# A windowed attention with sinks and a max-out FFN on one core: half-height score tiles, 32-wide sink tiles, crossbar transposes and another prologue

## The chip, the cores and the metric

The kernel runs on one core of a Trainium2 chip. The metric is the device time of one execution in microseconds (us). The engines are TensorE (PE; PEld is its weight load), VectorE (DVE), ScalarE (ACT), GpSimd (POOL) and SyncE (SP), which here only issues DMAs.

## The reference

```python
B, H, S, D = 4, 8, 768, 64            # n_sink = 4, window = 128
scores = q @ k.T / sqrt(D)
keep = (pos_k < 4) | ((0 <= pos_q - pos_k) & (pos_q - pos_k < 128))
a = softmax(where(keep, scores, -1e9))
x = (a @ v) as [B*S, H*D]             # 3072 x 512
h = max(x @ w1, x @ w2, x @ w3)       # each w is 512 x 768
out = h @ w_out                       # 768 x 512, float32
```

Inputs and output are float32; the kernel multiplies in bf16. No maximum is subtracted before the exp, and the sum over a row comes from a column of ones beside V.

## The kernel before, in words

The work is cut into 12 chunks of 256 query rows with all 8 heads, three chunks for each batch (`c` = 0, 1, 2). A chunk passes these steps, each a function with a letter in the order strings of `run` (L333):

- `load` (L59): four 256 KB DMAs of K and Q halves and four 128 KB DMAs of V, all on SP. `cast_qk` (L163) and `cast_v` (L171) make bf16 of them, on POOL but for the first two chunks.
- K and Q (`prep`, L185): 16 TensorE transposes (L192) into PSUM. Q is copied by ACT (L195), K by DVE (L200) into `kb`, a block-diagonal form: for two heads, 64 keys each, 128 rows and columns with zeros off the diagonal. The zeros are written once by `zeros` (L94), mostly on POOL. For the first chunk of a batch, small DVE copies (L208) put the four sink keys into `ks`.
- S (`score`, L214): eight tiles of 128 x 512 a chunk, a matmul of 128, one of 256 and one of 128 columns for each, an exp by ACT (L232), and for every second tile a multiplication by a 0/1 mask on DVE (L234). Z (`sink_score`, L236): four matmuls of 256 columns added into one tile, in chunks with c > 0.
- A (`av`, L249): for each half of the heads and each 128 queries one matmul for the sinks (260 columns) and eight of 130 columns (L263), against a V that is padded with zeros for the other head. DVE normalises (L268, L271). The sinks' V rows come from eight small DMAs (L84) and POOL products (L154).
- T (`xpose`, L276): four TensorE transposes of x for each 128 rows (L282) and an ACT copy (L283).
- F (`ffn_h`, L287): nine groups a chunk, each eight matmuls of 256 columns (L294); the first of three weights is copied by ACT (L298), the others are maximised in by DVE (L300).
- Y (`ffn_y`, L302): six matmuls of 512 columns (L305), an ACT copy (L308) and a DMA to the output on SP (L310), twice a chunk.

Every engine works through its instructions in the order of the program text, SP too. The first chunks (L339 to L377) have an order written out by hand; weights are loaded by POOL's queue, three matrices together for a range of columns, between POOL's casts and memsets. Then a loop over i = 2 to 11 (L379) casts chunk i+2, loads chunk i+3 and runs one string, which mixes the FFN of chunk i, the attention of chunk i+1 and the K and Q transposes of chunk i+2:

```python
run("Sb0 Fa0 Sb1 Kc0 Fa1 Sb2 Kc1 Fa2 Sb3 Fa3 Zb Sb4 Fa4 Ab00 Sb5 Fa5 Ab01 Sb6 Qc0 Fa6 "
    "Sb7 Qc1 Fa7 Fa8 Ab10 Ab11 Ya0 Tb0 Tb1 Ya1", a=i, b=i + 1, c=i + 2)
```

PSUM has two banks for scores, two for transposes and AV, four for the FFN.

Of the kernel before, what the change touches and what calls it, by code (L numbers as in the profile page):

```python
# [15 lines left out]
def kernel(  # L17
# [12 lines left out]
):  # L30
    nc = tc.nc
# [14 lines left out]

    with tc.manual_schedule():
        const = tc.alloc_tile_pool(name="const", bufs=1)  # L50
        raw = tc.alloc_tile_pool(name="raw", bufs=2)
        work = tc.alloc_tile_pool(name="work", bufs=2)
        ps_s = tc.alloc_tile_pool(name="ps_s", bufs=2, space=bass.MemoryType.PSUM)
        ps_o = tc.alloc_tile_pool(name="ps_o", bufs=2, space=bass.MemoryType.PSUM)
        ps_f = tc.alloc_tile_pool(name="ps_f", bufs=4, space=bass.MemoryType.PSUM)

        raws = {}

        def load(ci, gate=None):  # L59

            b, c = divmod(ci, CPB)
            t0 = c * 256
            eng = nc.sync
            qk = raw.tile([128, 2, H, 2, D], F32, tag="qk_raw", name="qk_raw")
            vr = raw.tile([128, 2, NP, 2, D], F32, tag="v_raw", name="v_raw")
            if gate is not None:
                gate.memset(qk[0:1, 0, 0, 0, 0:1], 0.0)
            for g in range(2):
                for j, src in ((0, k), (1, q)):
                    eng.dma_start(  # L70
                        out=qk[:, j, 4 * g:4 * g + 4],
                        in_=src[b, 4 * g:4 * g + 4, t0:t0 + 256].rearrange("h (p i) d -> p h (i d)", i=2))
            for h in range(2):
                for n in range(2):
                    eng.dma_start(
                        out=vr[64 * h:64 * h + 64, n],
                        in_=v[b, h::2, t0 + 128 * n:t0 + 128 * n + 128]
                            .rearrange("a (r i) d -> r a (i d)", i=2))
            raws[ci] = (qk, vr)

        load(0)
        vs_raw = const.tile([H * n_sink, B, D], F32, name="vs_raw")
        for h in range(H):
            nc.sync.dma_start(out=vs_raw[h * n_sink:(h + 1) * n_sink],  # L84
                              in_=v[:, h, 0:n_sink].rearrange("b s d -> s b d"))


        kb_sb = [const.tile([128, CPB, 2, NP, 2, 128], BF16, name=f"kb{i}") for i in range(2)]
        qT = [const.tile([128, NP, S], BF16, name=f"qT{i}") for i in range(2)]
        vb_sb = [const.tile([128, CPB, 2, NP, 2, 2, D + 1], BF16, name=f"vb{i}") for i in range(2)]  # L90
        ks = [const.tile([128, NP * 136], BF16, name=f"ks{i}") for i in range(2)]
        vs = const.tile([128, B, H, D + 1], BF16, name="vs")

        def zeros(i, c, eng):  # L94
            for h in range(2):
                hp = slice(64 * h, 64 * h + 64)
                eng.memset(kb_sb[i][hp, c, :, :, :, 64 - 64 * h:128 - 64 * h], 0.0)  # L97
                eng.memset(vb_sb[i][hp, c, :, :, :, 1 - h], 0.0)
                eng.memset(vb_sb[i][hp, c, :, :, :, h, D:D + 1], 1.0)

        zeros(0, 0, nc.vector)
        nc.vector.memset(ks[0], 0.0)
        nc.vector.memset(ks[1], 0.0)

        ident = const.tile([128, 128], BF16, name="ident")
        make_identity(nc, ident)

        msk = const.tile([128, 2, 4, 128], BF16, name="msk")
        nc.gpsimd.memset(msk[:, :, 0:2], 1.0)
        for h in range(2):  # L110
            hp = slice(64 * h, 64 * h + 64)
            nc.gpsimd.affine_select(
                out=msk[hp, :, 1], in_=msk[hp, :, 1], compare_op=ALU.is_ge, fill=0.0,
                base=0, pattern=[[-1, 2], [1, 128]], channel_multiplier=-2)
            nc.gpsimd.affine_select(
                out=msk[hp, :, 0], in_=msk[hp, :, 0], compare_op=ALU.is_gt, fill=0.0,
                base=0, pattern=[[1, 2], [-1, 128]], channel_multiplier=2)
        nc.gpsimd.tensor_copy(msk[:, :, 2:4], msk[:, :, 0:2])
        msk0 = const.tile([128, 2, 3, 128], BF16, name="msk0")
        nc.gpsimd.tensor_copy(msk0, msk[:, :, 1:4])  # L120
        for h in range(2):
            nc.gpsimd.memset(msk0[64 * h:64 * h + n_sink // 2, :, 0:2], 1.0)

        w_sb = {}

        def load_w(fo, fn):
            for wi, w in enumerate((moe_w1, moe_w2, moe_w3)):
                wt = const.tile([128, DS, fn], BF16, name=f"w{wi}_{fo}")
                nc.gpsimd.dma_start(
                    out=wt, in_=w[:, fo:fo + fn].rearrange("(a p) f -> p a f", p=128))  # L130
                for f in range(fn // 128):
                    w_sb[wi, fo // 128 + f] = wt[:, :, f * 128:(f + 1) * 128]

        wo = const.tile([128, FB, d_model], BF16, name="wo")

        def load_wo():
            for a in range(2):
                nc.gpsimd.dma_start(
                    out=wo[:, 3 * a:3 * a + 3],
                    in_=moe_w_out[384 * a:384 * a + 384].rearrange("(a p) f -> p a f", p=128))  # L140


        R = H * n_sink
        bm = const.tile([R, H], F32, name="bm")

        def sink_v_init():
            nc.gpsimd.memset(bm, 1.0)
            nc.gpsimd.affine_select(out=bm, in_=bm, compare_op=ALU.is_ge, fill=0.0, base=0,
                                    pattern=[[-n_sink, H]], channel_multiplier=1)
            nc.gpsimd.affine_select(out=bm, in_=bm, compare_op=ALU.is_ge, fill=0.0,  # L150
                                    base=n_sink - 1, pattern=[[n_sink, H]], channel_multiplier=-1)
            nc.gpsimd.memset(vs, 0.0)

        def sink_v(b):  # L154
            nc.gpsimd.tensor_tensor(
                out=vs[0:R, b, :, 0:D],
                in0=vs_raw[:, b].unsqueeze(1).to_broadcast([R, H, D]),
                in1=bm.unsqueeze(2).to_broadcast([R, H, D]), op=ALU.mult)
            nc.gpsimd.tensor_copy(vs[0:R, b, :, D:D + 1], bm.unsqueeze(2))

        bfs = {}

        def cast_qk(ci, j, g, eng):  # L163
            qk = raws[ci][0]
            if ci not in bfs:
                bfs[ci] = raw.tile([128, 2, 2, 2, 256], BF16, tag="qk_bf", name="qk_bf")
            eng.tensor_copy(  # L167
                bfs[ci][:, j, g].rearrange("p i (h d) -> p h i d", d=D),
                qk[:, j, 4 * g:4 * g + 4])

        def cast_v(ci, h):  # L171
            b, c = divmod(ci, CPB)
            vr = raws[ci][1]
            hp = slice(64 * h, 64 * h + 64)
            nc.gpsimd.tensor_copy(  # L175
                vb_sb[b % 2][hp, c, :, :, :, h, 0:D].rearrange("p n a i d -> p (n a i) d"),
                vr[hp].rearrange("p n a i d -> p (n a i) d"))

        def cast(ci):
            for j, g in ((0, 0), (1, 0), (0, 1), (1, 1)):  # L180
                cast_qk(ci, j, g, nc.gpsimd)
            for h in range(2):
                cast_v(ci, h)

        def prep(ci, j, g):  # L185

            b, c = divmod(ci, CPB)
            x = bfs[ci]
            pt = ps_o.tile([128, 2, 2, 128], BF16, tag="o", name="pt")
            for i in range(2):  # L190
                for p in range(2):
                    nc.tensor.transpose(pt[:, i, p], x[:, j, g, i, p * 128:(p + 1) * 128], ident)  # L192
            if j == 1:
                dst = qT[b % 2][:, 2 * g:2 * g + 2, c * 256:c * 256 + 256]
                nc.scalar.copy(dst.rearrange("p a (t i) -> p i a t", i=2), pt)  # L195
            else:
                kb = kb_sb[b % 2]
                for h in range(2):
                    hp = slice(64 * h, 64 * h + 64)
                    nc.vector.tensor_copy(  # L200
                        kb[hp, c, :, 2 * g:2 * g + 2, :, 64 * h:64 * h + 64]
                            .rearrange("p i a n r -> p i (a n) r"),
                        pt[hp].rearrange("p i a (n r) -> p i (a n) r", r=64))
                if c == 0:
                    kv = ks[b % 2].rearrange("p (a y) -> p a y", y=136)
                    for h in range(2):
                        for i in range(2):
                            nc.vector.tensor_copy(  # L208
# [215 lines left out]
```

## Time and profile before

| | us |
|---|---|
| median of 3 runs | 236.91 (236.32 to 238.7) |
| span of the profiled execution | 235.6 |
| PE busy | 203.3 |
| DVE busy | 140.4 |
| ACT busy | 115.1 |
| POOL busy | 91.8 |

The profile is one execution; its times count from the start of its span. Besides the page, this text uses four views. The groups of instructions give, for one line of the kernel and one operation, the busy time, the mean duration of one, and the idle time ahead of them with what ended it. The chain of waits is the sequence of work that ended last, followed back from the end: start, length, engine, tile and line. The timeline lists the instructions of one engine or queue: start, length, engine, line, operation, with the wait ahead of it in brackets. The table by stage lists for a stretch of time the busy time of PE, PEld, DVE, ACT and POOL, then the granted TensorE clock, the busy share of the DMA engines and GB/s. Matmuls overlap each other in time, so the spacing of their starts, and not the mean duration, is what one costs.

### The profile page before, as it was taken

To read this page: it belongs to the slowest core of one execution; us is meant where nothing else is said; L and a number is where in the kernel's file an instruction comes from. 1 tells how busy PE (TensorE), PEld (TensorE's weight loads), DVE (VectorE), ACT (ScalarE), POOL (GpSimd) and SP (SyncE) were. 2 spreads that over 40 slices of the span, in tenths; PEclk is the share of its full clock that TensorE was granted. 3 is DMA by queue.
4 is the path that set the end of the run, shared out by engine and by line. 5 is a ranking of instruction groups with operands and counts; after the bars stand their busy time and mean duration, and the time that the engine had idled before them with its cause. 6 is when DMAs were issued, how large, how long until landed. Compare 5 with 4: busy or idle time off the path is not lost.

```text
span 235.6 us, 4953 instructions
## 1 busy us (share of the span) xinstructions
PE 203.3 (86%) x1956; PEld 163.9 (70%) x1968; DVE 140.4 (60%) x314; ACT 115.1 (49%) x213; POOL 91.8 (39%) x129
## 2 busy tenths in 40 slices
PE   0647876989944999999899999998999999999993
PEld 0434655877533868978778869877978689799781
DVE  7737674456342973855856739729629648547350
ACT  2622363257450457546446555464564466473411
POOL 8599961699468650621602502603404300000000
PEclk9999999999997999999999999999999999999998
DMA  6599199682699904907607519139039020010202
GB/s 171 101 134 239 32 161 259 118 120 58 182 278 233 232 18 142 218 3 234 122 22 236 105 63 266 30 101 251 10 107 248 4 89 4 25 66 0 92 0 89
DMA packets 46006, 28.66 MB, mean 122 GB/s; under 512 B 2208, under 2 KB 42912, under 8 KB 45984
## 3 DMA queue, kind: packets, MB, share of 16 engines
q1 hardware_dynamic: 42016, 25.21, 43.4%
q0 software_dynamic: 3968, 3.15, 9.0%
q8 instruction: 15, 0.25, 0.5%
q14 instruction: 7, 0.06, 0.1%
HBM read 25.20 MB, written 6.29 MB: 134 GB/s over the span
## 4 chain that ended last, share of the span: by engine, by line
PE 57%; DVE 13%; POOL 9%; DMA 7%; ACT 5%; issue 4%; SPq 3%; POOLq 0%; DVEq 0%; ACTq 0%
PE h_ps L294 29%; PE y_ps L305 10%; PE o_ps L263 6%; DMA v_raw<-in_v_dram 4%; DVE e_sb L234 4%; DVE h_sb L300 4%; DMA w<-in_moe_w_dram 3%; PE st L224 3%; ACT e_sb L232 3%; PE pt L192 2%; DVE kb L200 2%; PE xt_ps L282 2%; POOL vb L175 2%; SPq L70 2%; POOL kb L97 2%
## 5 line engine op out<-in xcount | busy, mean ns | idle before, releaser
L294 PE MATMUL h_ps<-xT,w 128*128 128x256 bf16 x864 | 111.0, 278 | 2.2 <-DMA w<-in_moe_w_dram 1.5
L294 PEld LDWEIGHTS <-w 128*128 128x128 bf16 x864 | 82.7, 100 | 13.1 <-DMA w<-in_moe_w_dram 2.0
L232 ACT ACTIVATE e_sb<-st 128x512 bf16<-128x512 f32 (+1 forms) x96 | 53.5, 564 | 44.2 <-PE st L226 44.2
L234 DVE TENSOR_TENSOR e_sb<-e_sb,msk 128x1024 bf16<-128x1024 bf16 (+1 forms) x48 | 36.6, 762 | 56.0 <-ACT e_sb L232 55.9
L300 DVE TENSOR_TENSOR h_sb<-h_sb,h_ps 128x512 bf16<-128x512 bf16 x72 | 49.3, 685 | 15.6 <-PE h_ps L294 13.3
L167 POOL CAST qk_bf<-qk_raw 128x512 bf16<-128x512 f32 x40 | 24.9, 627 | 82.0 <-DMA qk_raw<-in_k_dram 71.1
L263 PE MATMUL o_ps<-vb,e_sb 128*128 128x130 bf16 x352 | 30.8, 227 | 6.8 <-DVE e_sb L234 4.0
L305 PE MATMUL y_ps<-wo,h_sb 128*128 128x512 bf16 x132 | 32.7, 379 | 0.6
L263 PEld LDWEIGHTS <-e_sb 128*128 128x128 bf16 x352 | 24.8, 100 | 10.5 <-DVE e_sb L234 6.2
L308 ACT COPY y_sb<-y_ps 128x512 f32<-128x512 f32 x24 | 14.0, 585 | 35.6 <-PE y_ps L305 32.1
L175 POOL CAST vb<-v_raw 64x1024 bf16<-64x1024 f32 x24 | 26.5, 1104 | 9.5 <-DMA v_raw<-in_v_dram 6.1
L192 PE MATMUL pt<-ident,qk_bf 128*128 128x128 bf16 x192 | 19.4, 230 | 12.1 <-DVE qk_bf L167 5.5
L298 ACT CAST h_sb<-h_ps 128x512 bf16<-128x512 f32 x36 | 21.1, 585 | 15.8 <-PE h_ps L294 15.6
L224 PE MATMUL st<-qT,kb 128*128 128x256 bf16 x96 | 27.0, 285 | 1.6 <-ACT qT L195 0.8
L200 DVE COPY kb<-pt 64x512 bf16<-64x512 bf16 x48 | 20.1, 419 | 6.9 <-PE pt L192 6.3
L192 PEld LDWEIGHTS <-qk_bf 128*128 128x128 bf16 x192 | 13.6, 102 | 14.4 <-POOL qk_bf L167 7.1
L195 ACT COPY qT<-pt 128x512 bf16<-128x512 bf16 x24 | 17.7, 737 | 11.5 <-PE pt L192 11.5
L226 PE MATMUL st<-qT,kb 128*128 128x128 bf16 x96 | 21.9, 228 | 0.0
L271 DVE TENSOR_TENSOR x_sb<-o_ps,rc 128x256 bf16<-128x256 f32 x48 | 20.4, 425 | 1.7
L305 PEld LDWEIGHTS <-h_sb 128*128 128x128 bf16 x144 | 13.0, 98 | 11.9 <-DVE h_sb L300 1.2
L283 ACT COPY xT<-xt_ps 128x512 bf16<-128x512 bf16 x24 | 13.2, 595 | 9.0 <-PE xt_ps L282 9.0
L222 PE MATMUL st<-qT,kb 128*128 128x128 bf16 x64 | 14.0, 218 | 0.9 <-ACT qT L195 0.8
(43 smaller groups left out, 130.7 us busy)
## 6 DMA issues: line engine op xcount, KB each, us to landing
qk_raw<-in_k_dram SPq DMA_DIRECT2D x24, 256.0 KB
qk_raw<-in_q_dram SPq DMA_DIRECT2D x24, 256.0 KB
v_raw<-in_v_dram SPq DMA_DIRECT2D x48, 128.0 KB
out_dram<-y_sb SPq DMA_DIRECT2D x24, 256.0 KB
w<-in_moe_w_dram POOLq DMA_DIRECT2D x3, 512.0 KB, 7.4
w<-in_moe_w_dram POOLq DMA_DIRECT2D x3, 256.0 KB, 4.9
wo<-in_moe_w_out_dram POOLq DMA_DIRECT2D x2, 384.0 KB, 5.6
vs_raw<-in_v_dram SPq DMA_DIRECT2D x8, 4.0 KB
```

The source lines that it names most:

```text
L167: eng.tensor_copy(bfs[ci][:, j, g].rearrange("p i (h d) -> p h i d", d=D), qk[:, j, 4 * g:4 * g + 4])
L175: nc.gpsimd.tensor_copy(vb_sb[b % 2][hp, c, :, :, :, h, 0:D].rearrange("p n a i d -> p (n a i) d"), vr[hp].rearrange("p n a i d -> p (n a ...
L192: nc.tensor.transpose(pt[:, i, p], x[:, j, g, i, p * 128:(p + 1) * 128], ident)
L200: nc.vector.tensor_copy(kb[hp, c, :, 2 * g:2 * g + 2, :, 64 * h:64 * h + 64] .rearrange("p i a n r -> p i (a n) r"), pt[hp].rearrange("p i ...
L224: nc.tensor.matmul(st[:, 1:3], lhsT=kb[:, c, i, p, 0], rhs=qh[:, q0:q0 + 256], start=True, stop=True)
L226: nc.tensor.matmul(st[:, 3], lhsT=kb[:, c, i, p, 1], rhs=qh[:, q0 + 128:q0 + 256], start=True, stop=True)
L232: nc.scalar.activation(e[:, i, lo:], st[:, lo:], AF.Exp, scale=scale)
L234: nc.vector.tensor_mul(e[:, :, lo:], e[:, :, lo:], msk if c > 0 else msk0)
L263: nc.tensor.matmul(o[:, 2 * a:2 * a + 2], lhsT=es[ci, p][:, i, sl], rhs=vb_sb[b % 2][:, n // 2, n % 2, p, i], start=(c == 0 and x == 0), s ...
L294: nc.tensor.matmul(hp[:, f], lhsT=w_sb[wi, 2 * fp + f][:, ds], rhs=xTs[ci][:, ds, :], start=(ds == 0), stop=(ds == DS - 1))
L300: nc.vector.tensor_max(dst, dst, hp)
L305: nc.tensor.matmul(yp, lhsT=hs[ci][:, fb, t * 128:(t + 1) * 128], rhs=wo[:, fb], start=(fb == 0), stop=(fb == FB - 1))
```

## The change

- K is no longer padded. `kT` holds 128 rows (two heads of 64) and 128 keys; a score tile is for one head and uses 64 of the 128 rows of the array, the two heads of a pair one after the other in the two halves. The number of tiles, exps and masks stays. V is no longer padded either: AV is a matmul of 65 columns for each head, query half and key block, 32 (c > 0) a chunk as before.
- The sinks stand in four column strips of 32: the sink scores of a pair of heads go to their own 32 partitions, and AV's sink matmuls read eight rows of such a strip. The sinks' V rows come from V by a selection matmul.
- Three DMAs load a chunk (K, Q, V of 512 KB each); `raw` and `work` have three buffers, and PSUM is one pool of eight banks that all tiles use in turn.
- K and Q of chunks 0 and 1 are transposed by TensorE from float32, those of chunks 2 and 3 from bf16; from chunk 4 on `turn_xbar` has SP issue DMA transposes, two for K and one for Q. From chunk 4 on x is transposed by two DMAs (`xpose_xbar`), which SP issues as well.
- The prologue works on two chunks. The weights are requested matrix by matrix, starting after the first part of chunk 1's K has landed, and the FFN of chunks 0 and 1 goes matrix by matrix too. A few matmuls on zeros are put at the start.
- The loop runs over i = 4 to 11. AV of chunk i+1 opens it, the scores of chunk i+2 follow four FFN groups, and y is that of chunk i-1. A y tile is stored by two DMAs.

The core of the diff (added lines, shortened):

```python
+    KQ_XBAR = 4
+    X_XBAR = 4
...
+        def turn32(ci, t, g, eng):
+            pt = bank([128, 2, 2, 128], F32, f"{t}t32")
+            x = raws[ci][t]
+            for a in range(2):
+                for i in range(2):
+                    for h in range(2):
+                        nc.tensor.matmul(pt[64 * h:64 * h + 64, a, i],
+                                         lhsT=x[:, 2 * (2 * g + a) + h, i], rhs=id32,
+                                         start=True, stop=True, skip_group_check=True)
...
+        def turn_xbar(ci):
+            x = bfs[ci, "k"].rearrange("p a i h d -> p (a i h d)")
+            for n in range(2):
+                nc.sync.dma_start_transpose(
+                    out=kT[ci % 4][:, n].rearrange("p a i r -> p (a i) r"),
+                    in_=x[64 * n:64 * n + 64])
+            nc.sync.dma_start_transpose(
+                out=qT[ci % 3].rearrange("p a i n r -> p (a i) (n r)"),
+                in_=bfs[ci, "q"].rearrange("p a i h d -> p (a i h d)"))
...
+        def sink_score(ci):
...
+            for p in range(NP):
+                nc.tensor.matmul(st[32 * p:32 * p + 32], lhsT=ks[b % 2][:, p],
+                                 rhs=q_ap(ci, p, None), start=True, stop=True,
+                                 skip_group_check=True)
...
+        def score(ci, p):
...
+            for what in range(lo, 4):
+                if what == 2:
+                    continue
                 for h in range(2):
                     hp = slice(64 * h, 64 * h + 64)
+                    kk = kT[(ci - (what == 0)) % 4][hp, int(what != 1), p].rearrange("p i r -> p (i r)")
+                    qq = q_ap(ci, p, {0: 0, 1: None, 3: 1}[what])[hp]
...
+                    nc.tensor.matmul(o, lhsT=kk, rhs=qq, start=True, stop=True)
...
+        def av(ci, pairs, eng=None):
...
+            if c:
+                for t in range(2):
+                    for p in pairs:
+                        pp = slice(32 * p, 32 * p + 2 * n_sink)
+                        nc.tensor.matmul(o[p][:, t], lhsT=es[ci, "sink"][pp, t], rhs=vs[b % 2][pp],
+                                         start=(t == 0), stop=False, skip_group_check=True)
+            for p in pairs:
...
+                        for h in range(2):
+                            nc.tensor.matmul(
+                                o[p][:, t, h], lhsT=es[ci, p][:, h, s],
+                                rhs=vb[(CPB * b + n // 2) % 4][:, n % 2, 2 * p + h],
+                                start=first, stop=(s == 2 * t + 1), skip_group_check=True)
...
+        def xpose_xbar(ci):
+            for t in range(2):
+                nc.sync.dma_start_transpose(
+                    out=xT_of(ci)[:, :, t * 128:(t + 1) * 128],
+                    in_=xs[ci][:, t].rearrange("p h d -> p (h d)"))
...
+        def attend(ci):
...
+            av(ci, range(NP))
+            if ci >= X_XBAR:
+                xpose_xbar(ci)
...
+        cast(3)
+        load_all(4)
+        for n in range(5):
+            F(2, n)
+        scores(3)
+        cast(4)
+        load_all(5)
+        turn_xbar(4)
+        F(2, 5)
...
+        attend(3)
+        ffn_y(2, 0)
+        T(3)
+        ffn_y(2, 1)
+        cast(5)
+        load_all(6)
+        turn_xbar(5)
+        scores(4)
...
+        for i in range(4, NCH):
             attend(i + 1)
             if i + 2 < NCH:
                 cast(i + 2)
             load_all(i + 3)
+            for n in range(4):
+                F(i, n)
+            if i + 2 < NCH:
+                turn_xbar(i + 2)
+            scores(i + 2)
+            ffn_y(i - 1, 0)
+            masks(i + 2, [0])
+            ffn_y(i - 1, 1)
+            masks(i + 2, [1])
+            F(i, 4)
+            masks(i + 2, [2])
+            F(i, 5)
+            masks(i + 2, [3])
+            F(i, 6)
+            F(i, 7)
+            F(i, 8)
+        ffn_y(NCH - 1, 0)
+        ffn_y(NCH - 1, 1, last=True)
```

`load_all(ci)` issues the three loads of a chunk, `cast(ci)` the eight casts on POOL, `scores(ci)` the sink scores and the four pairs' scores (ahead of them, for chunks below 4, the TensorE transposes), `F(i, n)` one FFN group, `masks` the multiplications by the mask. Chunk 2's load is held by `gate` and `wait_for` until the first part of the third FFN weight has landed.

## The prediction

> **What bounds the kernel now.** I read the page's busy shares first, then the groups of instructions, the chain that ended last, and last the timeline of single queues in the loop.
>
> ```profile
> PE 203.3 (86%) x1956; PEld 163.9 (70%) x1968; DVE 140.4 (60%) x314; ACT 115.1 (49%) x213; POOL 91.8 (39%) x129
> PEclk9999999999997999999999999999999999999998
> q1 hardware_dynamic: 42016, 25.21, 43.4%
> L294 PE MATMUL h_ps<-xT,w 128*128 128x256 bf16 x864 | 111.0, 278 | 2.2 <-DMA w<-in_moe_w_dram 1.5
> ```
>
> TensorE is the bound, and all DMAs of SP lie on one queue, q1. It is busy 43.4% of 235.6 us, 102 us, for 25.21 MB: 247 GB/s while it works. Matmuls overlap, so I take spacings from the chain of waits: eight FFN matmuls of 256 columns last 0.87 us (0.109 each), eight of 128 or 130 columns 0.46 (0.057), six y matmuls 1.30.
>
> ```profile
> 104.55 0.61 PE xt_ps L282 x8
> 121.92 0.45 PE xt_ps L282 x8
> 154.43 0.45 PE xt_ps L282 x8
> 172.02 0.45 PE xt_ps L282 x8
> 204.30 0.45 PE xt_ps L282 x8
> 219.69 0.45 PE xt_ps L282 x8
> ```
>
> This piece closes an iteration of the loop. From 104.55 to 204.30 six of them (chunks 4 to 9) take 99.75 us, 16.6 each. TensorE's own work for a chunk that is not first in its batch is 72 x 0.109 = 7.85 (FFN), 2.6 (y), 8 x 0.223 = 1.78 (scores), 0.44 (sink scores), 2.3 (AV), 0.46 (x) and 0.92 (K, Q) = 16.35. So the loop is dense. With about 1.7 us of y and copies behind 104.55, the span splits into 106.3 up to that loop, 99.8 in it and 29.5 behind.
>
> The early part has the idle time, and one of its stalls shows what the change will meet again:
>
> ```profile
> 73.83 0.61 PE L192 MATMUL pt<-ident,qk_bf 128*128 128x128 bf16 x4 [4.41 <-POOL qk_bf L167]
> 74.23 1.92 PE L294 MATMUL h_ps<-xT,w 128*128 128x256 bf16 x8
> 79.02 1.04 PE L294 MATMUL h_ps<-xT,w 128*128 128x256 bf16 x8
> ```
>
> ```profile
> 72.00:74.00 2.00, 0.17 (x2) 0.17 (x3) 0.00 (x0) 0.00 (x0) 2.00 (x5) 0.95 1.23 257
> 74.00:75.00 1.00, 1.00 (x8) 0.82 (x7) 0.51 (x2) 0.00 (x0) 0.88 (x2) 0.50 1.24 164
> 76.00:77.00 1.00, 1.00 (x9) 0.88 (x8) 0.76 (x2) 0.49 (x1) 0.38 (x1) 0.50 1.24 176
> 77.00:78.00 1.00, 1.00 (x11) 0.86 (x10) 0.77 (x2) 0.00 (x0) 0.88 (x1) 0.90 1.18 261
> ```
>
> After a wait of 4.41 us the granted clock (third column from the right) is 0.50 for three microseconds: eight matmuls take 1.92 instead of 1.04, and about 1.5 us go on top of the wait.
>
> ```profile
> 107.57 0.39 SPq L70 DMA_DIRECT2D qk_raw<-in_k_dram  x1
> 110.76 0.61 POOL L167 CAST qk_bf<-qk_raw 128x512 bf16<-128x512 f32 x1 [9.07 <-DMA qk_raw<-in_k_dram]
> 112.64 0.61 POOL L167 CAST qk_bf<-qk_raw 128x512 bf16<-128x512 f32 x1 [0.47 <-DMA qk_raw<-in_k_dram]
> 114.24 0.61 POOL L167 CAST qk_bf<-qk_raw 128x512 bf16<-128x512 f32 x1 [0.98 <-DMA qk_raw<-in_q_dram]
> 115.35 2.56 POOL L175 CAST vb<-v_raw 64x1024 bf16<-64x1024 f32 x2 [0.50 <-DMA v_raw<-in_v_dram]
> ```
>
> A chunk's load (1.57 MB) lands in the order of its issue: the first piece 2.8 us after its issue ends at 107.96, the last 7.7 us after the first issue. And SP issues in program order: it waits 129 us in all for y copies, with the loads queued behind them.
>
> **The change, part by part.**
>
> *Early part.* The block-diagonal K goes, and with it POOL's memsets (10 x 0.96, 10 x 0.97, 10 x 0.19: 21 us); the eight small sink loads (4.9 us of SP) and POOL's sink products (4.7) go too. FFN weights are requested right after chunk 1's first half, so the 7.4 us wait for w in the chain shrinks. What is new: 64 fp32 transposes for chunks 0 and 1, which no row shows. Bounds are the 128-column spacing 0.057 and, for operands twice as wide in several passes, 0.32 (above the 512-column 0.216); I take 0.16, nearer the short row, since half an output tile is written at a time: 10 us, partly under loads. Chunk 0's fourth piece lands at 8.33 (a DVE wait), so at 0.9 to 1.0 us a piece chunk 1's Q lands at 12 to 13. Two more transposes, a copy and a score bring FFN to 19 us, where the first weights (4.5 to 9.3 us after issue at about 11) are there too; bounds 15 and 25. From there to the y tiles of chunk 1: 18 FFN groups 15.7, y 5.2, scores 3.2, AV 3.8, transposes 1.8 = 29.7, and 2 for gaps: 51. On to chunk 4's loop: FFN 15.7, y 2.6, scores 4.2, AV 2.9, transposes 1.4 = 26.8, and 3 for the first crossbar chunk, whose request lies behind load 5: 81 us, against 106.3. Bounds 71 and 90.
>
> *Scores, sinks, AV.* A score tile costs 0.223 as before if its two 64-row halves follow each other, half if they run side by side: 1.78 or 0.9 a chunk, taken at 1.3; sink scores 0.44 or 0.1, taken at 0.3. AV halves its columns but keeps all 32 weight loads: 2.3 or 1.0, taken at 1.9. The Trainium skill, page "TensorEngine Tiling (Array Packing)", section Key Properties, speaks against it: changing the tiling mode drains the engine. No row here has such a switch; at an assumed 0.2 us for six switches a chunk the sum would be 14 us longer, without it as given here.
>
> *K, Q and x by DMA.* TensorE loses 0.92 + 0.46 a chunk, DVE the K copies (4 x 0.42), ACT 2 x 0.74 + 2 x 0.60. Neither is the bound: in the loop ACT keeps nine exps of 0.4 to 0.6, three h and two y copies (8 us), DVE four masks, six maxima and four normalisations (9.5). SP gains five issues a chunk, two more y stores and loses five load issues. The order on SP in iteration i is: x(i+1) twice, load i+3, K(i+2) twice and Q(i+2), then y stores; TensorE's is AV(i+1), four FFN groups, scores(i+2), y, five FFN groups. Counted from the start of AV:
> - x(i+1) is normalised at 3.3: DVE ends its last max at 0.9, then four times 0.176 + 0.425. SP, waiting for it, has load, K and Q behind it.
> - The x requests end at 4.4 (0.5 each, the load row; y stores show 0.36), the load lands at 4.4 + 7.7 = 12.1.
> - K and Q, 0.52 MB behind it on q1, need 2.1 at q1's 247 GB/s: 14.2. The low bound is no queueing: issues end at 7.6, plus 2.8, is 10.4. The high bound is a crossbar several times slower than a copy, 3 us or more for each 256 KB. The copy row is the nearest, as the bytes and the queue are the same.
> - TensorE reaches the scores at 1.9 + 4 x 0.87 = 5.4 and waits 8.8, twice the stall above: the clock halves, 1.5 more.
> - Behind it: sinks and scores 1.6, y 2.6, five FFN groups 4.4 = 8.6.
>
> T = 14.2 + 8.6 + 1.5 = 24.3. Five iterations (4 to 8) 121.5; iteration 9 loads nothing: 6.0 + 2.8 = 8.8, T = 8.8 + 8.6 + 0.8 = 18.2. Together 139.7, against 99.8.
>
> Two pages differ on the crossbar. "Advanced Engine Details and Errata", section X-Bar Transpose (TRN2), has it as fast as a plain copy, 350 to 400 GB/s: the sum would be 3 us shorter. "VectorE: DVE Perf Modes", section The three transpose paths, gives 1309 ns for a 128x128 block: as an estimate, 16 blocks one after the other are 21 us behind the load, and the sum passes 340.
>
> *Casts.* POOL's 4.7 us a chunk stay (V in four pieces), one iteration ahead of need: nothing, while the load lands before the next iteration's start.
>
> *End.* Iteration 10: AV 1.9, FFN 7.85, y 2.6; iteration 11: 10.45, then y 2.6 and the 3.5 us from the last matmul to the end: 28.9, against 29.5.
>
> **Sum.** 81 + 139.7 + 28.9 = 249.6, against the profile's span of 235.6; the median of the runs shown lies 1.3 above that span: 251 us.
>
> **Rivals.**
> 1. *Faster: K and Q do not queue behind the load's data.* Then they land at 10.4, T = 20.5, and 81 + 102.5 + 18.2 + 28.9 + 1.3 = 232. For it: SP has issued them by 7.6, and the load leaves the queue idle half of each period. Against: the landing order above. It decides at a landing by 10.9 us; with the low bounds of early part, scores and AV and no drop of the clock it gives 71 + 5 x 18.4 + 16.8 + 27.5 + 1.3 = 209.
> 2. *Slower still: the crossbar is the bound.* At 3 us for each 256 KB (x, K, Q) instead of 1.05, six iterations take 4 to 6 us more: 280. For it: no row shows a 2-byte transposing transfer; against: the bytes are only a third of the load's.
> 3. *The half tiles do not run side by side, or the switches cost:* 0.5 to 1.2 us a chunk over twelve chunks: 257 to 265. For it: the number of weight loads stays, and scores lie behind the wait, where nothing hides them; against: AV lies ahead of it and would be hidden.
>
> **How the numbers follow.** About 1% is what a measurement of this kernel can tell from no change. My forecast has 0.50 (own range 240 to 260; 0.48 slower, 0.02 the same). Rival 1 has 0.34 (0.30 faster, 0.04 the same), since the gain ahead of the loop, 25 us, is safe and the loss rests on one queue's order. Rival 2 has 0.11, rival 3 0.05 (0.04 slower, 0.01 the same). That is 0.30, 0.07 and 0.63. The range 219 to 263 leaves out rival 1's lowest and most of rival 2.
>
> **What would show it.** Right: iterations of 22 to 26 us in which TensorE waits 7 to 10 us ahead of the scores, for a DMA of kT or qT issued behind x and the load, with a granted clock of 0.5 behind the wait; FFN starting near 19 us; loop 4 starting near 81. Wrong: score matmuls that start without a wait, iterations under 19 us, or the wait on another engine. If x is ready well before 3.3, or SP issues the load ahead of it, the forecast falls.

## The result, and the profile after

| | before | after |
|---|---|---|
| median, us | 236.82 (236.32 to 238.7) | 272.5 (271.53 to 274.65) |
| ratio to before, 95% interval | | 1.1511 [1.144, 1.1582] |
| span of the profiled execution | 235.6 | 269.6 |
| PE busy | 203.3 | 186.8 |
| loop: first AV of iteration 4 | | 85.0 |
| six iterations 4 to 9 | 99.8 | 154.6 |

The kernel is 15% slower. The direction and the place were predicted; the forecast, 251, was 21.5 us too low, and the measured time lies outside its range (219 to 263). Two of the runs below, e6 and e7, were profiled in an execution that was slower than others of the same kernel, so their profiles are not used to compare times of iterations.

The page of the kernel after: busy shares, clock by slices, the load queue, the FFN group, and the transposing DMAs (issuer, count, median us to landing).

```profile
PE 186.8 (69%) x1934; PEld 138.2 (51%) x1946; DVE 115.1 (43%) x251; ACT 90.8 (34%) x177; POOL 64.3 (24%) x130
PEclk9999999999999965995599579757975798699998
q1 hardware_dynamic: 67152, 31.34, 52.3%
L352 PE MATMUL h_ps<-xT,w 128*128 128x256 bf16 x864 | 99.1, 273 | 1.2 <-ACT xT L335 1.1
...
kT<-k_bf SPq DMA_TRANSPOSE x16, 4.5
xT<-x_sb SPq DMA_TRANSPOSE x16, 2.5
qT<-q_bf SPq DMA_TRANSPOSE x8, 3.4
```

TensorE has 16.5 us less work and is idle 83 us. The first 14 slices (94 us) have a full clock; the dips begin with the loop. The waits of TensorE say where (total us, times, longest):

```profile
PE sk L254 <- DMA qT<-q_bf: 42.5, 6, 11.6
PE st L279 <- DMA qT<-q_bf: 22.2, 2, 11.4
```

64.7 us in eight waits, all for the transposed Q; the two shortest, 1.4 and 0.8 us, lie ahead of the loop. One iteration (i = 6, AV starts at 139.75), TensorE's timeline and then SP's, with the cast on POOL that starts when V has landed:

```profile
139.75 0.29 PE L302 MATMUL o_ps<-vs,e_sink 8*128 8x130 bf16 x8
...
140.99 3.66 PE L352 MATMUL h_ps<-xT,w 128*128 128x256 bf16 x32
155.28 0.41 PE L254 MATMUL sk<-qT,ks 128*32 128x256 bf16 x4 [10.64 <-DMA qT<-q_bf]
155.62 1.89 PE L279 MATMUL st<-qT,kT 64*128 64x128 bf16 x24
...
160.47 4.53 PE L352 MATMUL h_ps<-xT,w 128*128 128x256 bf16 x40
164.93 0.29 PE L302 MATMUL o_ps<-vs,e_sink 8*128 8x130 bf16 x8
```

```profile
142.80 2.54 SPq L339 DMA_TRANSPOSE xT<-x_sb  x2
145.39 0.58 SPq L78 DMA_DIRECT2D k_raw<-in_k_dram  x1
146.02 0.57 SPq L78 DMA_DIRECT2D q_raw<-in_q_dram  x1
146.64 1.12 SPq L78 DMA_DIRECT2D v_raw<-in_v_dram  x1
147.85 3.85 SPq L217 DMA_TRANSPOSE kT<-k_bf  x2
151.80 1.34 SPq L220 DMA_TRANSPOSE qT<-q_bf  x1
153.53 2.62 POOL L181 CAST vb<-v_raw 64x512 bf16<-64x512 f32 x4 [0.71 <-DMA v_raw<-in_v_dram]
```

SP has nothing to issue until x is ready, 3.05 us after the start of AV, and then issues without a break for 10.3 us; Q's request is out 13.4 us after the start of AV, Q lands at 15.5, and TensorE has stood still since 4.9. The table by stage shows what the wait does to the clock (third column from the right):

```profile
145.00:148.00 3.00, 0.00 (x0) 0.00 (x0) 0.00 (x0) 0.26 (x1) 0.00 (x0) 1.00 0.49 106
148.00:149.00 1.00, 0.00 (x0) 0.00 (x0) 0.00 (x0) 0.00 (x0) 0.00 (x0) 0.55 1.15 346
149.00:153.00 4.00, 0.00 (x0) 0.00 (x0) 0.00 (x0) 0.00 (x0) 2.34 (x4) 0.50 1.25 289
156.00:157.00 1.00, 1.00 (x20) 0.88 (x18) 0.00 (x0) 0.86 (x3) 0.14 (x1) 0.50 0.06 16
158.00:159.00 1.00, 0.78 (x5) 0.38 (x4) 0.71 (x2) 1.00 (x3) 0.00 (x0) 0.83 0.00 0
```

It halves 3.5 us into the wait and comes back 3 us after its end, so the 24 score matmuls take 1.89 us (1.06 in runs below where the clock behind the wait is 1.00).

### The profile page after: what moved, and what is told of

Read it like the earlier page. It is cut to its first block, busy times and chain, and to the rows that moved or that the text cites. A ratio compares the mean times of both kernels' runs of the same rounds, so it can differ in the third digit from the quotient of the medians.

```text
span 269.6 us, 4874 instructions
## 1 busy us (share of the span) xinstructions
PE 186.8 (69%) x1934; PEld 138.2 (51%) x1946; DVE 115.1 (43%) x251; ACT 90.8 (34%) x177; POOL 64.3 (24%) x130
## 4 chain that ended last, share of the span: by engine, by line
PE 54%; DMA 25%; SPq 6%; DVE 5%; ACT 5%; issue 3%; POOL 1%; ACTq 0%; DVEq 0%; POOLq 0%
PE h_ps L352 27%; DMA q_raw<-in_q_dram 14%; PE y_ps L363 13%; DMA qT<-q_bf 10%; PE st L279 5%; SPq L339 4%; PE o_ps L311 3%; ACT e_sb L281 3%; PE kt L200 2%; PE qt L200 2%; DVE e_sb L287 2%; DVE h_sb L358 1%; DMA k_raw<-in_k_dram 1%; SPq L78 1%; SPq L217 1%
## 5 line engine op out<-in xcount | busy, mean ns | idle before, releaser
L352 PE MATMUL h_ps<-xT,w 128*128 128x256 bf16 x864 | 99.1, 273 | 1.2 <-ACT xT L335 1.1
L352 PEld LDWEIGHTS <-w 128*128 128x128 bf16 x864 | 83.5, 98 | 13.4 <-issue 2.1
L281 ACT ACTIVATE e_sb<-st 128x512 bf16<-128x512 f32 (+1 forms) x96 | 45.6, 586 | 27.3 <-PE st L279 26.9
L287 DVE TENSOR_TENSOR e_sb<-e_sb,msk 128x1024 bf16<-128x1024 bf16 x32 | 21.8, 696 | 58.1 <-ACT e_sb L281 58.0
L178 POOL CAST k_bf<-k_raw 128x512 bf16<-128x512 f32 x20 | 11.9, 622 | 112.8 <-DMA k_raw<-in_k_dram 97.4
L181 POOL CAST vb<-v_raw 64x512 bf16<-64x512 f32 x48 | 30.5, 636 | 18.3 <-DMA v_raw<-in_v_dram 16.3
L279 PE MATMUL st<-qT,kT 64*128 64x128 bf16 (+1 forms) x256 | 17.7, 293 | 24.1 <-DMA qT<-q_bf 22.2
L363 PEld LDWEIGHTS <-h_sb 128*128 128x128 bf16 x144 | 15.2, 112 | 21.9 <-issue 11.9
L279 PEld LDWEIGHTS <-kT 64*128 64x128 bf16 x256 | 11.8, 117 | 28.4 <-issue 26.2
L369 ACT COPY y_sb<-y_ps 128x512 f32<-128x512 f32 x23 | 13.6, 601 | 17.7 <-PE y_ps L363 13.2
L311 PE MATMUL o_ps<-vb,e_sb 128*128 128x65 bf16 x352 | 14.9, 194 | 3.3 <-DVE e_sb L287 2.8
L311 PEld LDWEIGHTS <-e_sb 128*128 128x128 bf16 x352 | 12.4, 97 | 5.7 <-DVE e_sb L287 3.9
L178 POOL CAST q_bf<-q_raw 128x512 bf16<-128x512 f32 x18 | 10.8, 629 | 6.4 <-DMA q_raw<-in_q_dram 6.4
L289 DVE TENSOR_TENSOR e_sb<-e_sb,msk 128x768 bf16<-128x768 bf16 x16 | 10.1, 651 | 4.6 <-ACT e_sb L281 4.6
```

The lines of the kernel that those rows point to most:

```text
L178: eng.tensor_copy(bfs[ci, t][:, :, i], x)
L181: eng.tensor_copy(vb[ci % 4][64 * i:64 * i + 64, n, :, 0:D], raws[ci]["v"][64 * n:64 * n + 64, :, i])
L279: nc.tensor.matmul(o, lhsT=kk, rhs=qq, start=True, stop=True)
L281: nc.scalar.activation(e[:, h, lo:], st[h][:, lo:], AF.Exp, scale=scale)
L287: eng.tensor_mul(e, e, msk)
L311: nc.tensor.matmul(o[p][:, t, h], lhsT=es[ci, p][:, h, s], rhs=vb[(CPB * b + n // 2) % 4][:, n % 2, 2 * p + h], start=first, stop=(s == 2 ...
```

## The experiments

The theory (A): what costs is the order on SP, x, then the load, then K and Q, because K and Q are needed first. The rivals: (B) the crossbar itself is too slow, or the queue that all share; (C) the half tiles and the narrow tiles cost TensorE more than they save. T below is the distance of two AV starts in the loop. Ratios are against runs of the kernel before in the same series; a diff is against the kernel after. The edits are shown shortened. T is left out for e6 and e7.

| run | median us | ratio to before | T, iterations 5 to 8 |
|---|---|---|---|
| after | 272.5 | 1.1511 [1.144, 1.1582] | 25.2 to 27.2 |
| e1_load_behind | 252.63 | 1.0671 [1.0557, 1.0784] | 21.7 to 22.9 |
| e2_kq_first | 206.08 | 0.8705 [0.8564, 0.8846] | 13.3 to 14.4 |
| e7_kq_first_all | 202.16 | 0.8567 [0.8512, 0.8623] | |
| e10_earlier_scores | 202.88 | 0.8557 [0.8492, 0.8622] | 13.2 to 14.5 |
| e3_x_on_tensor | 228.91 | 0.9689 [0.9622, 0.9755] | 18.7 to 20.5 |
| e4_kq_on_tensor | 213.3 | 0.901 [0.8966, 0.9053] | 14.7 to 15.2 |
| e5_no_xbar | 219.03 | 0.9252 [0.9096, 0.9408] | 15.3 to 15.8 |
| e8_load_on_act_queue | 277.21 | 1.1733 [1.1653, 1.1813] | 25.3 to 27.3 |
| e6_dummies_in_wait | 270.87 | 1.1375 [1.1272, 1.1478] | |
| e9_dummies_longer | 266.01 | 1.1192 [1.1098, 1.1285] | 23.6 to 25.6 |

**The load behind K and Q.**

```
             attend(i + 1); cast(i + 2)
-            load_all(i + 3)
             F(i, 0..3)
             turn_xbar(i + 2)
+            load_all(i + 3)
```

> In the loop the three loads of chunk i+3 are issued behind the K and Q transposes of chunk i+2 instead of ahead of them; nothing else moves. Theory A (K and Q come late because SP issues x, then the load, then K and Q, and the load's data lies ahead on q1): iterations 4 to 8 become like iteration 9 of the changed kernel, which loads nothing: K and Q ready 11.3 us after the start of AV instead of 15.4, iterations of 21.6 instead of about 26, some 20 us less, 252. Theory B (the crossbar or the queue is simply too slow for three transposes a chunk, whatever the order): within 3 us of 272. Theory C (the half tiles and mode switches cost TensorE the time): 272.

252.6, as expected. In its timeline (AV starts at 133.29) SP issues x, K and Q one behind the other:

```profile
136.34 2.55 SPq L339 DMA_TRANSPOSE xT<-x_sb  x2
138.99 2.53 SPq L217 DMA_TRANSPOSE kT<-k_bf  x2
141.62 1.26 SPq L220 DMA_TRANSPOSE qT<-q_bf  x1
...
144.97 0.41 PE L254 MATMUL sk<-qT,ks 128*32 128x256 bf16 x4 [6.79 <-DMA qT<-q_bf]
```

Q is ready 11.7 us after the start of AV instead of 15.5, and K's two requests take 2.53 instead of 3.85. So the load ahead of K and Q costs 3.8 us an iteration: 2.4 in which SP issues it, and 1.3 more for K's requests. Of the wait, 6.8 us remain with no load in front.

**K and Q ahead of x and of the load.**

```
+            cast(i + 2)
+            turn_xbar(i + 2)
             attend(i + 1)
-            cast(i + 2)
             load_all(i + 3)
             F(i, 0..3)
-            turn_xbar(i + 2)
             scores(i + 2)
```

> In the loop the casts and the K and Q transposes of chunk i+2 stand ahead of AV of chunk i+1 in the program, so that SP issues them before it waits for x; loads stay behind x. Theory A: K and Q are ready about 6 us after AV starts, TensorE hardly waits for them (0 to 1.5 us), iterations of 14 to 16 us instead of 25, the total 205 to 215. Theory B: the wait moves to x or to the next K and Q, iterations stay above 20 us, the total above 245. Theory C: iterations without a wait, but TensorE busy longer than the 13.2 us that its spacings give; total above 225.

206, as expected: every DMA is still there and all bytes still cross the same queue, only SP's order differs. The iteration whose AV starts at 103.12, and the start of the next:

```profile
101.83 3.47 SPq L217 DMA_TRANSPOSE kT<-k_bf  x2
105.40 1.25 SPq L220 DMA_TRANSPOSE qT<-q_bf  x1
106.75 2.54 SPq L339 DMA_TRANSPOSE xT<-x_sb  x2
108.83 0.29 PE L254 MATMUL sk<-qT,ks 128*32 128x256 bf16 x4 [1.30 <-DMA qT<-q_bf]
...
117.22 0.29 PE L302 MATMUL o_ps<-vs,e_sink 8*128 8x130 bf16 x8
```

K's requests leave while TensorE is still at the FFN ahead of AV. x goes out 3.6 us after the start of AV and is not needed before the next iteration's FFN; the load comes last. The wait is 1.3, T is 14.1. (B) is refuted: the same crossbar and the same queue carry an iteration in 14 us.

**The prologue's two loads behind K and Q too** (e7: e2, and `turn_xbar(4)` ahead of `load_all(5)`, `turn_xbar(5)` ahead of `load_all(6)`).

> The version with K and Q ahead of x in the loop, and in the part before the loop the transposes of chunk 4 ahead of load 5 and those of chunk 5 ahead of load 6. Theory A: the scores of chunk 4 lose their wait of 1.5 us and the K transposes issue in 1.3 us each instead of 2.7; the masks and exps still set the pace there, so 1 to 4 us less than 206: 202 to 205. Theory B: no change or worse.

202.2, as expected, though the interval overlaps that of e2, so that a gain over e2 is not shown. The two waits for qT that the kernel after has ahead of its loop, 1.4 and 0.8 us, are gone in e7's profile. With e10 this is the fastest kernel of the study.

**No crossbar for K and Q (e4), for x (e3), for either (e5).** `KQ_XBAR = 12` and the `turn_xbar` calls removed; `X_XBAR = 12` with `T(4)` behind `F(3, 5)` and `T(i + 1)` behind the four FFN groups; both.

> K and Q of all chunks are transposed by TensorE (16 matmuls and two PSUM copies a chunk, as for chunks 2 and 3); x stays with the crossbar. Theory A: no wait ahead of the scores, no fall of the clock; the iteration is TensorE's 13.2 + 0.9 + up to 1.5 for the copies, 14 to 16 us; the waits between 57 and 82 us go as well (about 10 us); total 195 to 210. Theory B, with the crossbar left with x alone: the same, so this run does not tell A from B. Theory C: above 225.

> x of all chunks is transposed by TensorE; K and Q stay with the crossbar, behind the load as in the changed kernel. SP then waits for nothing ahead of the load, so it issues it right behind the y stores, some 7 us earlier than now. Theory A: K and Q are ready at about 8 us after the start of AV instead of 15.4; TensorE waits 2 to 4 us, the clock holds in most iterations, iterations of 16 to 18 us, total 220 to 230. Theory B (the crossbar is too slow for K and Q): the wait stays above 8 us, total above 255.

> K, Q and x of all chunks are transposed by TensorE; the rest of the change stays (unpadded K, 64-row score tiles, 32-wide sinks, two-chunk prologue). Theories A and B: like the run with K and Q alone on TensorE, plus 0.5 us of transposes and up to 1 us of copies an iteration: 195 to 215, so the rest of the change is worth over 20 us by itself. Theory C: no better than the kernel before, 230 or more.

213, 229 and 219. Two came out a little above what (A) gave (213 for 195 to 210, 219 for 195 to 215). The miss is not in the loop: T is 14.7 to 15.2 in e4, for 14 to 16 expected, with the wait for a copy of Q on ACT (1.1 us) in it. It lies ahead of the loop, where 10 us were to go: the first AV comes at 90.2 and 90.6, later than the 85.0 of the kernel after. (C) is refuted: e5 has every half tile, every narrow sink tile and none of the crossbar, is 7.5% faster than before, and its T is 15.3 to 15.8 against 16.6 before. Most of its gain lies ahead of the loop, though (90.6 against 106.3). Its timeline has the prices:

```profile
116.62 0.29 PE L254 MATMUL sk<-qT,ks 128*32 128x256 bf16 x4 [1.23 <-ACT qT L191]
116.84 1.06 PE L279 MATMUL st<-qT,kT 64*128 64x128 bf16 x24
```

A chunk's 24 score matmuls take 1.06 us where eight tiles at 0.223 took 1.78. And e3 shows that x ahead of K and Q is not the whole of it: without x on the queue the load still goes first, and TensorE still waits for qT (15.0 us in four waits at the sink scores and 4.1 in one more, up to 5.4 each where 2 to 4 were expected). Its total is as expected, but its T, 18.7 to 20.5, is above the 16 to 18 that was expected.

**The loads on ACT's queue, beside SP's.** The prediction said that K and Q lie behind the load *on q1*. Here SP issues x, K and Q, and ACT issues the load, behind the four FFN groups.

```
             attend(i + 1); cast(i + 2)
-            load_all(i + 3)
             F(i, 0..3)
+            load_all(i + 3, nc.scalar)
             turn_xbar(i + 2)
```

> The loop's loads are issued by ACT's queue, behind the copy of the fourth FFN group, which is within half a microsecond of when SP issues them now; SP goes from x to K and Q at once. If the wait comes from SP's order and from q1 being served in order: K and Q ready near the 11.3 us of iteration 9, up to 12.5 with shared bandwidth, iterations of 22 to 23 us, total 253 to 259. If it comes from the bandwidth that load and transposes share, whichever queue they lie on: K and Q still at 14 to 15.5, total 267 to 272.

277, above either expectation. Of the 6.2 us between its profiled span (275.8) and that of the kernel after, 3.8 lie ahead of the loop, which the edit leaves as it was; T is that of the kernel after (25.3 to 27.3 against 25.2 to 27.2), so the loop gained nothing. One iteration (AV starts at 143.50), then the landing times of its page:

```profile
146.55 2.50 SPq L339 DMA_TRANSPOSE xT<-x_sb  x2
148.51 0.38 ACTq L78 DMA_DIRECT2D k_raw<-in_k_dram  x1
...
152.07 2.50 SPq L220 DMA_TRANSPOSE qT<-q_bf  x1
159.80 0.41 PE L254 MATMUL sk<-qT,ks 128*32 128x256 bf16 x4 [11.41 <-DMA qT<-q_bf]
```

```profile
kT<-k_bf SPq DMA_TRANSPOSE x16, 7.1
xT<-x_sb SPq DMA_TRANSPOSE x16, 2.5
qT<-q_bf SPq DMA_TRANSPOSE x8, 6.4
```

Q's request is out 11.1 us after the start of AV instead of 13.4, but it lands 5.2 us later instead of 2.1, at 16.3. x, which meets no load, lands in 2.5 as before. So the order on q1 alone is not what holds K and Q: the load delays them from another queue as well. The Trainium skill, page "DMA: Bandwidth & Descriptors", section Issuing engines are not separate DMA queues, says that transfers of all issuers run on the same 16 DMA engines and interleave, and that another issuer saves only the time to issue, usually small beside the transfer. The first half fits this run (a load issued by ACT delays SP's transposes from a landing of 2.1 us to 5.2); the second does not fit the loop after, where issuing takes SP 10.3 us an iteration and Q's landing 2.1 after it.

**Dummy matmuls in the wait.** Multiplications of zeros, their result unused, 75 and 45 of them (e6); then 95 and 60 (e9).

```
+            if i + 2 < NCH:
+                warm(75 if i + 3 < NCH else 45)
             scores(i + 2)
```

> The changed kernel with matmuls on zeros put into the loop's wait ahead of the scores: 75 of 256 columns (8.2 us of the 10.6 that TensorE waits), 45 in iteration 9. They end before K and Q are ready, so only the granted clock can change. If the fall of the clock costs what the prediction took (1.5 us an iteration), six iterations are 6 to 9 us shorter: 264 to 266. If the clock's fall is harmless because ACT's exps set the pace behind the wait: no difference, 271 to 274. If the matmuls delay the scores: longer than 274.

> The kernel after with 95 dummy matmuls of 256 columns (60 in the iteration without a load) ahead of each chunk's scores in the loop, on zeros, their result unused; at the 0.111 us each of the run with 75 they last 10.5 us and so end within about 1 us of the arrival of qT, where 75 left a gap of 2.8. If the granted clock that falls in the wait costs TensorE 1.5 us behind each of six waits, as the prediction has it: about 264 us, with a clock of 1.00 in the rows behind the wait. If what follows the wait is set by the exps and the maximum copies of ScalarE and VectorE and not by TensorE's clock: the clock is 1.00 all the same and the time stays at 270 to 273. If the dummies outlast the arrival, up to 275.

With 75 the result is unclear: 270.9, runs from 267 to 276, and in the profile gaps of 2.8 to 4.6 us were left in iterations 4 to 8, behind which the clock was 0.5 all the same. With 95 the time is 266.0 and its interval lies below that of after: 6.5 us, or 1.1 for each of the six waits where 1.5 was expected. Stretches of e9 behind a wait that ends at 156.13:

```profile
156.00:157.00 1.00, 0.87 (x22) 0.75 (x24) 0.00 (x0) 0.53 (x2) 0.95 (x2) 1.00 0.00 0
158.00:159.00 1.00, 1.00 (x7) 0.45 (x5) 0.71 (x2) 1.00 (x3) 0.00 (x0) 1.00 0.00 0
```

The clock is 1.00, and from the sink scores to the next AV 8.35 us pass (156.13 to 164.48) instead of 9.65. The clock's share of the loss is real and small; the wait is the rest.

**Scores of chunk 5 earlier** (on top of e7). Counted from `attend(4)` they move by two FFN groups, one of them because `attend(4)` itself moves back by one.

```
-        attend(4)
         F(3, 5)
-        F(3, 6)
+        attend(4)
         scores(5)
+        F(3, 6)
+        masks(5, [0])
         F(3, 7)
-        masks(5, [0, 1])
+        masks(5, [1])
         F(3, 8)
```

> K and Q issued ahead of load and x everywhere, as in the run of 202 us, and in the prologue attend(4) one FFN group later, scores(5) two groups earlier (directly behind attend(4)), its masks behind F(3,6), F(3,7) and F(3,8). If AV's waits for masks before the loop (three of 0.2 to 0.8 us for chunk 4 and four of 0.4 to 0.8 us for chunk 5) come from too little TensorE work between a chunk's scores and its AV, they shrink by 2 to 3 us together and the first AV of the loop starts at 82 to 83.5 instead of 85.3: 199 to 201 us. If they come from VectorE's or ScalarE's own load in that stretch: the waits move, the AV starts at 85 again, 202 to 203 us.

202.9, no gain, and the waits moved more than they shrank:

```profile
79.32 0.40 PE L279 MATMUL st<-qT,kT 64*128 64x128 bf16 x6 [0.41 <-DVE h_sb L358]
...
83.68 0.29 PE L302 MATMUL o_ps<-vs,e_sink 8*128 8x130 bf16 x8
...
84.83 0.42 PE L311 MATMUL o_ps<-vb,e_sb 128*128 128x65 bf16 x8 [0.50 <-DVE e_sb L287]
86.03 0.42 PE L311 MATMUL o_ps<-vb,e_sb 128*128 128x65 bf16 x8 [0.78 <-DVE e_sb L287]
87.04 0.42 PE L311 MATMUL o_ps<-vb,e_sb 128*128 128x65 bf16 x8 [0.59 <-DVE e_sb L287]
87.30 5.32 PE L352 MATMUL h_ps<-xT,w 128*128 128x256 bf16 x32
```

AV of chunk 5 starts at 83.7 instead of 85.0 in the kernel after, waits 1.9 us for its masks, more than the 1.1 there, and the score tiles now wait for DVE too. None of these waits is longer than 0.8 us, yet behind them the granted clock is 0.50 from 88 to 90 and the next 32 FFN matmuls take 5.32 us, where the kernel after needs 3.66; e2 shows the same 5.32 at this place, so it is not this edit that brings it. Too little TensorE work between scores and AV is not the cause, or not alone; whether DVE or ACT sets this stretch stays open.

## Why the prediction was right in direction and 21.5 us short

The profile splits the miss. Each line is measured against the prediction's own term:

| term | predicted | measured | miss |
|---|---|---|---|
| start of iteration 4 | 81 | 85.0 | 4.0 |
| iterations 4 to 8 | 5 x 24.3 = 121.5 | 28.0 + 26.75 + 25.2 + 25.9 + 27.2 = 133.0 | 11.5 |
| iteration 9 | 18.2 | 21.6 | 3.4 |
| end | 28.9 | 30.0 | 1.1 |
| median above the profiled span | 1.3 | 2.9 | 1.6 |
| sum | 251 | 272.5 | 21.5 |

**The step that failed: "The x requests end at 4.4", at "0.5 each, the load row".** A transposing request holds SP 1.25 us, not 0.5: x's pair 2.54, K's pair 2.54 where nothing interferes, Q 1.26 although it is twice as large. x was ready at 3.05 (predicted 3.3), but its requests end at 5.6. From there the prediction's own terms, 7.7 for the load and 2.1 for K and Q, give 15.4; iteration 6 measures 15.5. (The two terms are a little off in opposite ways, 8.2 until V has landed and 1.75 from there to Q.) Over iterations 4 to 8 Q is ready at 18.6, 15.9, 15.5, 15.8 and 16.0, a mean of 16.4 instead of 14.2, and that makes 10.8 of the 11.5 us. Of these, 8.3 lie ahead of the end of x's requests: it comes at 5.6 to 5.7 instead of 4.4, and at 7.8 in iteration 4, where AV's mask waits hold x as well. The other 2.5 lie behind it. What follows the wait was right: 10.2 on average for 8.6 + 1.5 = 10.1.

The same price shows bare in iteration 9, which has no load (AV starts at 217.98):

```profile
221.03 2.52 SPq L339 DMA_TRANSPOSE xT<-x_sb  x2
223.64 2.54 SPq L217 DMA_TRANSPOSE kT<-k_bf  x2
226.27 1.26 SPq L220 DMA_TRANSPOSE qT<-q_bf  x1
```

Issues end 9.55 us after the start of AV, Q lands at 11.5; the prediction had 6.0 + 2.8 = 8.8. That is 2.7 of this iteration's 3.4.

**The mechanism was half right.** That K and Q wait behind x and the load, and TensorE behind them, is what the trace and e1 and e2 show. "Behind the load on q1" is not: e8 took the load off q1 and gained nothing. The load costs 3.8 to 4 us of the wait (e1; 11.5 in iteration 9 against 15.5). In the kernel after these stand on SP, as the load's own issues and longer ones of K; in e8, where SP has no load to issue, they stand behind the requests, as a later landing. That fits bytes that share the DMA engines, but no run shows the sharing by itself. The larger part, the 6.8 us of wait that are left in e1, is five requests of 1.25 us that cannot start before x.

**The start of iteration 4.** The first FFN matmul came at 20.0 (19 predicted), the FFN of chunk 2 at 51.3 (51). Between 51.3 and 85.0 TensorE waits 5.9 us by its timeline (2.2 for the crossbar's Q, the rest for masks, x and a Q copy), where 3 were allowed, and works 27.8, where 26.8 were counted. The AV pieces that open the loop, just behind this stretch, show the kind:

```profile
85.01 0.55 PE L302 MATMUL o_ps<-vs,e_sink 8*128 8x130 bf16 x8
...
86.26 0.42 PE L311 MATMUL o_ps<-vb,e_sb 128*128 128x65 bf16 x8 [0.18 <-DVE e_sb L287]
87.46 0.42 PE L311 MATMUL o_ps<-vb,e_sb 128*128 128x65 bf16 x8 [0.78 <-DVE e_sb L287]
```

Still, the early part brought what was claimed of it: 85.0 against 106.3 before.

**The rivals.** Rival 1 (K and Q land by 10.4) does not happen even without any load: 11.5. Rival 2 gave 280 and is the nearest in time, and its condition is partly met: x and K hold SP 2.5 us for each 256 KB. But it put the price in the crossbar's rate, as a bound of the kernel, and e2 moves the same transposes in 14 us an iteration. The range should have reached to it; it was left out at a chance of 0.11, although no row showed a transposing request. Rival 3 is refuted by e5. Of the two prices for the crossbar that the prediction quotes, neither came out: the sum was neither 3 us shorter nor past 340. The estimates of TensorE's forms were too cautious: scores 1.06 (1.3 taken), AV with its sinks 1.24 (1.9 taken), sink scores 0.29 (0.3 taken). The drain at mode switches that the prediction weighed left no 14 us anywhere: e5's chunks with all switches are about 1 us shorter than those of before (15.3 to 15.8 against 16.6).

## What to carry to other kernels

When transfers share one issuing engine, list its program order with the issue time of each and the moment its data are ready: a request that must wait (here x) belongs behind those that are ready and needed sooner (K and Q). Here that order alone moved the same instructions from 272 to 202 us, from 15% slower to 14% faster. And when no row shows a kind of request, its issue time needs bounds of its own beside its bytes: x's two requests in every iteration, and all five where no load hides K's and Q's, at 1.25 us instead of 0.5 were what the forecast lacked.

## What the runs showed of the hardware

- A DMA transpose between two places in SBUF holds SP 1.25 us a request (128 KB of x, 1.19 to 1.26; 256 KB of Q, 1.24 to 1.78), up to 4.1 for a K piece beside loads; in the loop a plain load of 512 KB holds it 0.57 to 0.58 for K and Q, and 0.75 to 1.65 for the V behind them. Counted from the issue it lands no later than a plain copy: x's 128 KB in 2.5 us, y's stores of the same size in 2.4.
- The eight fp32 transposes of half a K (two records each) took 1.02 to 1.09 us, 0.13 each, where 0.16 was taken. The first two of these pieces took 1.73 and 1.89, though the granted clock reads 1.00 there too; why stays open.
- A chunk's 24 score matmuls take 1.06 us on 64 of the 128 rows each, and took 1.78 on all rows with the same columns: the two halves overlap, though not wholly.
- The granted clock halved 3.5 us into a wait of 10.6 (after, iteration 6), and also behind a row of mask waits of at most 0.8 us each (e2, e10). The same waits in the kernel after (0.18, 0.78 and 0.18) left it at 1.00, so the longest single wait does not decide alone; what else does, no run shows.
